# Weight conversion beside attention moved to fixed places in the program, its loads issued a period ahead, with a third raw buffer and two exchanged banks

## The chip, the core and the metric

The kernel runs on one core of a Trainium2 chip. The metric is the device time of one execution in microseconds. Three runs of the kernel before took 648.32, 651.28 and 651.58 us, median 651.28. The engines are TensorE (PE, with its weight loads shown apart as PEld), VectorE (DVE), ScalarE (ACT), GpSimd (POOL) and SyncE (SP), which issues nearly all DMAs.

## What is computed

An attention with a compressive memory feeds a gated feed-forward network (FFN). Cut to what matters:

```python
B, H, S, D = (4, 8, 576, 64)
scores = scale * q @ k^T;  causal mask;  a = softmax(scores)
local = a @ v
q_p = phi(q)                                   # phi(x) = elu(x) + 1
mem_out = (q_p @ M_prev) / (q_p . z_prev + 1e-6)
g = sigmoid(beta)                              # per head
x = g * mem_out + (1 - g) * local              # -> [2304 tokens, 512]
gate = x @ w_gate;  val = x @ w_val            # 512 -> 1536
out = (silu(gate) * val) @ w_out               # 1536 -> 512
```

Everything is float32, but the three weight matrices arrive as 64-bit floats, handed over as pairs of 32-bit words. The kernel makes 32-bit floats of them on the chip.

## The kernel before

**Attention.** Two heads form a pair, and there are 16 pairs. The loop runs n = 0 to 16; one turn is called a period here. Period n computes the scores of pair n in blocks of 128, 256, 384, 512 and 2 x 288 keys, takes row minima and exponentials of them (`exp`, ACT), and scales them (`weighed`, POOL). Beside it stands the second half of pair n-1: its weights are transposed on PE (`turned1`, `turned`; the transposed copies are called g), the memory is read (`recall`, result `mem` scaled by `w`), and values are summed (`recalled`, `values`). `leave` writes the result x in two parts: a rounded high part (`xh`, ACT) and the remainder (`xl`, DVE). q and k are split in the same way into `qh`, `ql`, `kh`, `kl`, and a product takes three matmuls (high x high, low x high, high x low). From the second pair on, `ql` and `kl` are made on POOL.

**Banks.** Four PSUM banks, s0 to s3, hold scores. Four others, tr0 to tr3, are taken in turn by `rot` for transposes, memory reads and the sums. In each period the last two takers are the pair of sums that `recalled` opens: one for token blocks 0 and 1 (`first`), one for the rest (`rest`). The sum that sits in tr2 and the one in tr3 are read by `leave` in the following period before the first long transposes (`turned(2, 0)` into tr2, `turned(2, 1)` into tr3) may overwrite them.

**Weights.** A third is a 128 x 512 piece of one weight matrix; there are 36, three (gate, value, out) for each of 12 slices f of the hidden dimension. A third is loaded raw (`raw_load`, tile `wraw`, 512 KB, two buffers), its upper words are taken through an activation (`raw_top`, ACT, tile `we`), two DVE operations make the bits of it (`we`, then `wa`), a third DVE operation joins the lower word (`wa<-wraw,wa`), ACT rounds the high part (`wgh` or `woh`) and DVE makes the low part (`wgl` or `wol`). Gate and value thirds are also written to `wdr`, out thirds to `wdo`, to be read again in the later passes. The first three thirds are made during attention, at EARLY = (1, 2, 3), the other 33 in the first pass of the FFN.

**What sets the order.** The lower-case engine names `pe, act, dve, pool` (made by `queued`) chain each instruction to the one before, so it stays in the order of the program text. Instructions on the upper-case names `ACT, DVE, SP` are placed by the framework's scheduler, by priorities. The thirds beside attention are on the upper-case names and are given a priority 200 later than their place in the text.

**FFN.** Three passes over 768 tokens each, t0 = 0, 768, 1536; a unit is one pass and one slice f, so 36 units. In the first pass a unit takes four products of 12 matmuls (`eight`), which take two banks in turn, and six groups of three (`lower`) that add the output. The two later passes use seven products. The functions that the change and the steps below touch are `raw_load`, `raw_top`, `low_part`, `third`, `pair_split`, `recalled`, the period loop and the loop over the units with its inner `some`.

Of the kernel before, what the change touches and what calls it, by code (L numbers as in the profile page):

```python
# [9 lines left out]
F32 = mybir.dt.float32  # L10
F32R = mybir.dt.float32r
I32 = mybir.dt.int32
AF = mybir.ActivationFunctionType
ALU = mybir.AluOpType
# [12 lines left out]

P_LOAD = 400
ORDER = (0, 768, 1536)
EARLY = (1, 2, 3)  # L30
P_EARLY = 200
ACT_K = (0, 1)
ON_POOL = ("q", "k")
PS_S, PS_T = 4, 4
# [9 lines left out]
def attention_moe(ctx: ExitStack, tc: tile.TileContext, qt, kt_, v, m, beta, wg, wv, wo, out):  # L44
# [61 lines left out]
        return pool.tensor_scalar(dst, src, 1.0, 0.0, op0=ALU.mult, op1=ALU.add)  # L106

    def split_lo(dst, src, hi, kind=""):
        eng = pool if kind in ON_POOL else DVE
        return eng.tensor_tensor(dst, src, hi.bitcast(F32), op=ALU.subtract)  # L110

    ident = const.tile([128, 128], F32, name="ident")
# [42 lines left out]

    held, wout = {}, {}
    thirds = [(f, j) for f in range(NF) for j in range(3)]
    raws, tops, low_parts = {}, {}, []

    def raw_load(n, after=None):  # L160
        if n < len(thirds):
            f, j = thirds[n]
            raws[n] = rot(wp, "wraw", [128, 512, 2], I32, 2)
            ld = SP.dma_start(raws[n].rearrange("p a b -> p (a b)"), (wg, wv, wo)[j][f].bitcast(I32))
            if after is not None:
                follow(ld, after, "the loads that the attention waits for go first")
# [11 lines left out]
                for i, o in enumerate((oh, ol)):  # L178
                    SP.dma_start(wdo[f, :, i], o.bitcast(F32))

    def third(act, dve, n):

        low_part(dve)
        if n >= len(thirds):
            return
        f, j = thirds[n]
        e, low = tops.pop(n), raws.pop(n)[:, :, 0]
        dve.tensor_scalar(e, e, W_TOP * 2.0**-111, -W_TOP * 2.0**-79, op0=ALU.min, op1=ALU.max)
        a = rot(wp, "wa", [128, 512], I32, 3)
        dve.tensor_scalar(a, e.bitcast(I32), 3, None, op0=ALU.logical_shift_left)  # L190
        dve.scalar_tensor_tensor(
            out=a, in0=low, scalar=29, in1=a, op0=ALU.logical_shift_right, op1=ALU.bitwise_or
        )
        if j == 0:
            held[f] = [rot(wp, f"wg{part}", [128, 1024], F32R, 2) for part in "hl"]
        if j == 2:
            wout[f] = oh, ol = [rot(wp, f"wo{part}", [128, 512], F32R, 3) for part in "hl"]
        else:
            c = slice(j * 512, j * 512 + 512)
            oh, ol = (x[:, c] for x in held[f])  # L200
            SP.dma_start(wdr[f, :, c], a.bitcast(F32))
        act.copy(oh, a.bitcast(F32))
        low_parts.append((f, j, a.bitcast(F32), oh, ol))

    with tc.tile_pool(name="sb", bufs=1, reuse_waits="tile") as sb:

# [17 lines left out]
        def pair_split(n, raw):  # L224
            qr, kr = raw
            q = [rot(sb, f"q{part}", [128, 640], F32R, NK) for part in "hl"]
            k = [rot(sb, f"k{part}", [128, 576], F32R, NK) for part in "hl"]
            early = n == 0
            (ACT.copy if n in ACT_K else split_hi)(k[0], kr)
            split_hi(q[0], qr[:, 128:768])  # L230

            def lows():
                split_lo(q[1], qr[:, 128:768], q[0], "" if early else "q")
                split_lo(k[1], kr, k[0], "" if early else "k")

            return q, k, lows

# [20 lines left out]
        class Pair:  # L258
# [128 lines left out]

            def recalled(self):

                rest, first = (rot(psT, "tr", [128, 512], F32, PS_T) for _ in range(2))  # L390
                self.av = first, rest
                y = self.mem.rearrange("p t j d -> p t (j d)")
                for t in (2, 3, 0, 1):
                    o = t % 2 * 128
                    pe.matmul(self.av[t // 2][:, o : o + 128], y[:, t], ident, start=(t % 2 == 0), stop=False, skip_group_check=True)
# [75 lines left out]
        pairs[0].load()  # L471
        gates()
        pairs[0].split()
        pairs[0].load_v()
        pairs[0].phi_parts()()
        pairs[1].load()
        pairs[0].lows()
        nothing = lambda *args: None
        ending = lambda: nothing
        for n in range(NP + 1):  # L480
# [25 lines left out]
            turned(2, 1, dve)  # L506
            exp(1, 1)
            scale = old.recall() if old else nothing
            if cur:
                cur.weighed(((0, 0), (0, 1), (1, 0), (1, 1)))  # L510
            scale()
            if after:
                after.lows()
            phi = after.phi_parts() if after else nothing
            reads = [scores(t) for t in range(2, 4)]
# [24 lines left out]
                    pairs[n + 2].load()  # L540
            if after:
                after.load_v()
            if n in EARLY:
                with later_by(P_EARLY):
                    i = EARLY.index(n)
                    raw_load(i, loads[n + 1])
                    raw_top(ACT, i)
                    third(ACT, DVE, i)
                    low_part(DVE)

        ending()()

# [1 line left out]
    with tc.tile_pool(name="stg2", bufs=1, reuse_waits="tile") as stg2, \  # L554
# [209 lines left out]
        first = units[0][0]  # L764
        for p, i, j in (("p1", 0, 0), ("p2", 0, 1), ("p7", 1, 0), ("p4", 1, 1)):
            direct(first, p, i, j)
        raw_load(3)
        raw_load(4)
        before = None
        spreads = lambda mix, *what: [  # L770
            (high if kind == "h" else low)(mix, p, k) for kind, p in what for k in range(2)
# [2 lines left out]
        for n, unit in enumerate(units):  # L774
# [5 lines left out]
            again(n)  # L780
            if whole and left:
                def some(i):
                    if i == 3:
                        raw_top(act, 3)
                    third(act, dve, i)
                    raw_top(act, i + 1)
                    raw_load(i + 2)
                for k in range(3):
                    plan[k].append(lambda i=3 * n + 3 + k: some(i))
            if n < len(units) - 1 and units[n + 1][0] != first:  # L790
# [106 lines left out]
```

## Time and profile before

| | before |
|---|---|
| median of three runs | 651.28 us |
| the profiled execution, its own time | 653.73 us |
| its span, first to last instruction | 651.8 us |
| PE busy | 627.0 us (96%) |
| DVE busy | 460.0 us (71%) |
| ACT busy | 362.7 us (56%) |
| POOL busy | 156.0 us (24%), all in the attention |
| mean granted PE clock | 0.988 |

Busy shares are means over two quite different stages: the attention ends at about 212 us, the FFN fills the rest. The end of a matmul is modelled, so a PE row can look longer than the engine was held; the starts are what to compare. A timeline row gives the start in us, the duration in us, the engine, the line, the operation, and in brackets how long the engine sat idle before it and what ended that. The granted clock is a share of full speed: 1.0 is 2.4 GHz, 0.5 is 1.2 GHz.

### The profile page before, as it was taken

The numbers are of one execution on the slowest core, as the hardware profiler recorded it, in microseconds if no ns is written. First come the engines' busy times: TensorE is split into PE (matmuls) and PEld (weight loads), VectorE is DVE, ScalarE is ACT, GpSimd is POOL, SyncE is SP. The second block draws the span as 40 slices with busy tenths as digits, with TensorE's granted clock in tenths as the row PEclk, the third lists the DMA queues.
The fourth block names the chain that finished last, engine by engine and source line by source line (L and its number), as shares of the span: only waits on it lengthen the run. The fifth ranks groups of instructions, "written<-read, shape, count | busy, mean of one in ns | idle before, by whom it ended". The sixth has DMA issues, their size and how long they took to land.

```text
span 651.8 us, 11300 instructions
## 1 busy us (share of the span) xinstructions
PE 627.0 (96%) x3912; PEld 558.4 (86%) x3912; DVE 460.0 (71%) x1151; ACT 362.7 (56%) x838; POOL 156.0 (24%) x217
## 2 busy tenths in 40 slices
PE   3889999999999899999999999999999999999997
PEld 2767878878787799999999999999999999999995
DVE  4878887878876567667686666665688756666653
ACT  6667887878874444434445565454445744445342
POOL 4667878878783000000000000000000000000000
PEclk9979999999999899999999999999999999999999
DMA  7466557554331676688765561222646533232102
GB/s 216 133 207 203 167 159 219 158 146 153 100 110 42 220 237 198 208 283 284 255 211 171 201 209 66 98 97 76 214 163 223 182 117 109 66 113 81 65 32 98
DMA packets 48744, 102.46 MB, mean 157 GB/s; under 512 B 6960, under 2 KB 16176, under 8 KB 48688
## 3 DMA queue, kind: packets, MB, share of 16 engines
q1 hardware_dynamic: 48544, 101.45, 48.0%
q8 instruction: 31, 0.51, 0.4%
q10 hardware_dynamic: 144, 0.29, 0.1%
q14 instruction: 25, 0.20, 0.1%
HBM read 74.99 MB, written 26.74 MB: 156 GB/s over the span
## 4 chain that ended last, share of the span: by engine, by line
PE 84%; DVE 5%; ACT 4%; DMA 4%; issue 2%; POOL 1%; DVEq 0%; SPq 0%; ACTq 0%; POOLq 0%
PE s L83 52%; PE tr L83 32%; ACT pl L83 3%; DMA wraw<-in_wo_dram 2%; ACT g L83 1%; DVE mem L83 1%; DMA wraw<-in_wg_dram 1%; DVE pl L83 1%; DVE w L83 1%; DMA qr<-in_qt_dram 1%; DVE rs L83 1%; POOL ps L83 0%; DMA out_dram<-pt 0%; POOL ql L83 0%; POOL kl L83 0%
## 5 line engine op out<-in xcount | busy, mean ns | idle before, releaser
L83 PE MATMUL tr<-woh,uh 128*128 128x512 f32 x144 | 57.3, 398 | 0.0
L83 PE MATMUL tr<-wol,uh 128*128 128x512 f32 x144 | 56.7, 394 | 0.0
L83 PE MATMUL tr<-woh,ul 128*128 128x512 f32 x144 | 56.5, 393 | 0.0
L83 POOL TENSOR_SCALAR pl<-pl,rs,og 128x384 f32<-128x384 f32 (+1 forms) x64 | 44.8, 715 | 29.8 <-DVE rs L83 23.8
L83 ACT ACTIVATE pl<-pl,mx 128x384 f32<-128x384 f32 (+1 forms) x64 | 42.4, 665 | 15.0 <-DVE mx L83 15.0
L83 ACT ACTIVATE zh<-zh 128x384 f32<-128x384 f32 x24 | 12.7, 530 | 67.8 <-DVE zh L83 67.8
L83 PE MATMUL tr<-g,vp 128*64 128x320 f32 (+4 forms) x448 | 48.7, 360 | 0.0
L83 PE MATMUL s<-kh,qh 64*128 64x128 f32 (+4 forms) x160 | 37.2, 389 | 11.2 <-ACT gs L142 6.9
L83 DVE TENSOR_TENSOR zv<-s,zv 128x384 f32<-128x384 f32 x24 | 13.4, 558 | 47.1 <-PE s L83 47.1
L83 PEld LDWEIGHTS tr<-g,vp 128*64 128x64 f32 x448 | 29.4, 137 | 16.9
L83 DVE CUSTOM_DVE_ANT_0 pl<-s,maskp 128x384 f32<-128x384 f32 (+1 forms) x64 | 38.1, 616 | 0.0
L83 POOL TENSOR_SCALAR ps<-ps,rs,og 128x128 f32<-128x128 f32 (+1 forms) x64 | 32.3, 518 | 14.4 <-DVE rs L83 14.0
L83 DVE COPY g<-tr 128x384 f32<-128x384 f32 (+1 forms) x64 | 32.1, 522 | 3.0 <-PE tr L83 1.8
L83 ACT ACTIVATE ps<-ps,mx 128x128 f32<-128x128 f32 (+1 forms) x64 | 28.8, 457 | 9.5 <-DVE mx L83 9.5
L83 ACT COPY g<-tr 128x384 f32<-128x384 f32 (+1 forms) x64 | 31.5, 529 | 4.3 <-DVE w L83 2.2
L83 PEld LDWEIGHTS tr<-ident,pl 128*128 128x128 f32 x224 | 24.7, 144 | 9.9 <-issue 7.3
L83 PEld LDWEIGHTS s<-kh,qh 64*128 64x128 f32 (+1 forms) x160 | 19.3, 198 | 16.2 <-issue 7.1
L83 PEld LDWEIGHTS tr<-woh,ul 128*128 128x128 f32 x144 | 27.1, 188 | 7.0 <-DVE ul L83 0.3
L83 DVE TENSOR_TENSOR tl<-tt,th 128x512 fp32r<-128x512 f32 x48 | 32.8, 684 | 0.0
L83 ACT CAST th<-tt 128x512 fp32r<-128x512 f32 x48 | 30.0, 624 | 4.8 <-DVE tt L83 2.0
L83 PE MATMUL tr<-ident,pl 128*128 128x128 f32 x224 | 32.0, 285 | 0.6 <-DVE xl L83 0.6
L83 PE MATMUL s<-kl,qh 64*128 64x128 f32 (+4 forms) x160 | 31.9, 334 | 0.7 <-DVE kl L110 0.6
(187 smaller groups left out, 1960.6 us busy)
## 6 DMA issues: line engine op xcount, KB each, us to landing
wr<-wdr SPq DMA_DIRECT2D x24, 512.0 KB, 3.3
qr<-in_qt_dram SPq DMA_DIRECT2D x16, 384.0 KB, 3.3
wraw<-in_wg_dram SPq DMA_DIRECT2D x12, 512.0 KB, 4.1
wdr<-wa SPq DMA_DIRECT2D x24, 256.0 KB, 2.7
wraw<-in_wv_dram SPq DMA_DIRECT2D x12, 512.0 KB, 3.9
wraw<-in_wo_dram SPq DMA_DIRECT2D x12, 512.0 KB, 4.5
wol<-wdo SPq DMA_DIRECT2D x24, 256.0 KB, 2.8
woh<-wdo SPq DMA_DIRECT2D x24, 256.0 KB, 3.2
```

Of the source, the lines that this page charges most:

```text
L83: ins = getattr(eng, name)(*args, **kw)
```

## The change

The conversion of a third is cut in pieces with places of their own. For the three thirds beside attention the load is issued in one period, the activation stands in the next, the two bit operations in the one after, the joining of the lower word and the high part one later, and the low part one later still, all on the chained engine names; they begin at EARLY = (2, 5, 8). Three more thirds (3, 4, 5) are loaded in periods 11, 12, 13, and the activation of third 3 is done in period 13; before, the loads of 3 and 4 stood after the attention and that activation in the first unit of the FFN. There are three raw buffers in place of two, and in the FFN loads run three thirds ahead in place of two.

In the opening, `kl` of pair 0 is made before `ql`, both stand ahead of the first phi and on the chained engine, and in period 0 the `ql` and `kl` of pair 1 go to POOL ahead of the scaling of the first blocks. In `recalled` the names `first` and `rest` are exchanged, so that `first` sits in tr2 and `rest` in tr3.

```diff
-EARLY = (1, 2, 3)
-P_EARLY = 200
+EARLY, AHEAD = (2, 5, 8), (11, 12, 13)
...
-            raws[n] = rot(wp, "wraw", [128, 512, 2], I32, 2)
+            raws[n] = rot(wp, "wraw", [128, 512, 2], I32, 3)
...
+    def third_bits(dve, n):
+        e = tops[n]
+        dve.tensor_scalar(e, e, W_TOP * 2.0**-111, -W_TOP * 2.0**-79, op0=ALU.min, op1=ALU.max)
+        wa[n] = a = rot(wp, "wa", [128, 512], I32, 3)
+        dve.tensor_scalar(a, e.bitcast(I32), 3, None, op0=ALU.logical_shift_left)
...
-            (ACT.copy if n in ACT_K else split_hi)(k[0], kr)
+            (act.copy if early else ACT.copy if n in ACT_K else split_hi)(k[0], kr)
...
             def lows():
+                if early:
+                    split_lo(k[1], kr, k[0])
                 split_lo(q[1], qr[:, 128:768], q[0], "" if early else "q")
-                split_lo(k[1], kr, k[0], "" if early else "k")
+                if not early:
+                    split_lo(k[1], kr, k[0], "k")
...
-                rest, first = (rot(psT, "tr", [128, 512], F32, PS_T) for _ in range(2))
+                first, rest = (rot(psT, "tr", [128, 512], F32, PS_T) for _ in range(2))
...
+            if n == 0:
+                after.lows()
             if cur:
                 cur.weighed(((0, 0), (0, 1), (1, 0), (1, 1)))
             scale()
-            if after:
+            if after and n:
                 after.lows()
...
-            if n in EARLY:
-                with later_by(P_EARLY):
-                    i = EARLY.index(n)
-                    raw_load(i, loads[n + 1])
-                    raw_top(ACT, i)
-                    third(ACT, DVE, i)
-                    low_part(DVE)
+            for i, at in enumerate(EARLY):
+                if n == at - 1:
+                    raw_load(i, loads[n + 2])
+                if n == at:
+                    raw_top(act, i)
+                if n == at + 1:
+                    third_bits(dve, i)
+                if n == at + 2:
+                    third_word(act, dve, i)
+                if n == at + 3:
+                    low_part(dve)
+            if n in AHEAD:
+                raw_load(len(EARLY) + AHEAD.index(n), loads[n + 2])
+                if n == AHEAD[-1]:
+                    raw_top(act, len(EARLY))
...
-        raw_load(3)
-        raw_load(4)
...
                 def some(i):
-                    if i == 3:
-                        raw_top(act, 3)
                     third(act, dve, i)
                     raw_top(act, i + 1)
-                    raw_load(i + 2)
+                    raw_load(i + 3)
```

DVE in period 0, from the reading of the 512-key scores (`pl<-s`) to the reciprocals of the sums (`rs`), before:

```order
L83 ISA pl_223,mx_149<-s_159,maskp 128x512
L188 TENSOR_SCALAR we_408<-we_408 128x512
L83 ISA pl_225,mx_149<-s_160,maskp 128x512
L190 TENSOR_SCALAR wa_411<-we_408 128x512
L83 ISA p_215,mx_149<-s_151,maskp 128x288
L191 SCALAR_TENSOR_TENSOR wa_411<-wraw_406,wa_411 128x512
L83 ISA p_215,mx_149<-s_152,mask_89,mx_149 128x288
L83 SCALAR_TENSOR_TENSOR ph_194<-qe_139,ph_194 128x640
L176 TENSOR_TENSOR wgl_415<-wa_411,wgh_414 128x512
L83 TENSOR_SCALAR rs_233<-sm_150 128x5
```

and now:

```order
L82 ISA pl_223,mx_149<-s_159,maskp 128x512
L82 ISA pl_225,mx_149<-s_160,maskp 128x512
L82 ISA p_215,mx_149<-s_151,maskp 128x288
L82 ISA p_215,mx_149<-s_152,mask_89,mx_149 128x288
L82 SCALAR_TENSOR_TENSOR ph_194<-qe_141,ph_194 128x640
L82 TENSOR_SCALAR rs_233<-sm_150 128x5
```

The four operations of the first third have left this place. They stand at the ends of periods 3, 4 and 5 now, each between the first `xl` of a period's end and the first reading of the next period's scores.

PE at the end of a period, from the transposes of the last block (`ident,p`) through the memory read (`ident,mem`) to the sums over values (`g,vp`), before:

```order
L83 MATMUL tr0_272<-ident_76,p40_215 128x128 x4
L83 MATMUL tr1_277<-ident_76,p40_215 128x128
L83 MATMUL tr2_284<-ident_76,mem0_295 128x128 x2
L83 MATMUL tr3_289<-ident_76,mem0_295 128x128 x2
L83 MATMUL tr3_289<-g10_247,vp0_132 64x256 x2
L83 MATMUL tr2_284<-ident_76,mem0_295 64x64 x2
L83 MATMUL tr2_284<-g20_248,vp0_132 64x320 x6
```

and now:

```order
L82 MATMUL tr0_272<-ident_76,p40_215 128x128 x4
L82 MATMUL tr1_277<-ident_76,p40_215 128x128
L82 MATMUL tr3_289<-ident_76,mem0_295 128x128 x2
L82 MATMUL tr2_284<-ident_76,mem0_295 128x128 x2
L82 MATMUL tr2_284<-g10_247,vp0_134 64x256 x2
L82 MATMUL tr3_289<-ident_76,mem0_295 64x64 x2
L82 MATMUL tr3_289<-g20_248,vp0_134 64x320 x6
```

The order of the matmuls is the same; tr2, which ACT empties into g just before, is now written second, and tr3, which DVE empties, first.

ACT at the start of the FFN, from its first gate activation (`zg`) to the second (`zh`), before:

```order
L83 ACTIVATE zg_2524<-s_152 128x384
L83 ACTIVATE we_566<-wraw_564 128x512
L83 CAST wgh_2530<-wa_411 128x512
L83 ACTIVATE we_408<-wraw_406 128x512
L83 CAST uh_2549<-zg_2524 128x384
L83 CAST wgh_2530<-wa_569 128x512
L83 ACTIVATE we_566<-wraw_564 128x512
L83 ACTIVATE zh_2573<-s_152 128x384
```

and now:

```order
L82 ACTIVATE zg_2527<-s_152 128x384
L82 CAST wgh_2532<-wa_701 128x512
L82 ACTIVATE we_553<-wraw_849 128x512
L82 CAST uh_2551<-zg_2527 128x384
L82 CAST wgh_2532<-wa_1137 128x512
L82 ACTIVATE we_993<-wraw_1285 128x512
L82 ACTIVATE zh_2575<-s_152 128x384
```

One activation (`we`) has left the stretch, and the two that remain read raw buffers that were loaded in periods 12 and 13.

## Rows read from the trace of the kernel before

**Rows 1.** Chain that ended last, shares of the span.
```profile
PE 84%; DVE 5%; ACT 4%; DMA 4%; issue 2%; POOL 1%; DVEq 0%; SPq 0%; ACTq 0%; POOLq 0%
```

**Rows 2.** Windows: stretch, its length, busy us of engines, granted clock, DMA.
```profile
33.70:51.15 17.45, 14.30 (x111) 11.60 (x107) 12.42 (x44) 11.07 (x31) 10.76 (x14) 0.80 0.62 197
63.17:203.24 140.07, 138.97 (x1261) 112.18 (x1262) 115.32 (x431) 109.80 (x310) 113.13 (x153) 1.00 0.48 144
220.55:223.77 3.22, 0.17 (x2) 0.00 (x1) 1.12 (x3) 1.25 (x3) 0.00 (x0) 0.85 0.76 263
223.77:229.66 5.89, 5.89 (x18) 5.89 (x19) 4.23 (x9) 2.38 (x5) 0.00 (x0) 0.50 0.79 258
```

**Rows 3.** Timeline of PE, periods 0 to 2, rows with a wait.
```profile
16.74 0.47 PE L83 MATMUL s<-kh,qh 64*128 64x128 f32 x2 [2.35 <-DVE mx L83]
39.47 2.54 PE L83 MATMUL tr<-mm,ph 128*128 128x130 f32 x10 [2.92 <-ACT g L83]
```

**Rows 4.** Timeline of DVE, periods 0 to 2.
```profile
15.36 0.62 DVE L188 TENSOR_SCALAR we<-we 128x512 f32<-128x512 f32 x1 [1.75 <-ACT we L171]
16.51 1.01 DVE L190 TENSOR_SCALAR wa<-we 128x512 int32<-128x512 int32 x1
20.20 0.16 DVE L83 TENSOR_SCALAR rs<-sm 128x5 f32<-128x5 f32 x1
...
31.17 1.49 DVE L176 TENSOR_TENSOR wgl<-wa,wgh 128x512 fp32r<-128x512 f32 x1
```

**Rows 5.** Timeline of ACT, periods 0 and 2.
```profile
14.66 0.67 ACT L171 ACTIVATE we<-wraw 128x512 f32<-128x512 f32 x1 [0.55 <-DMA wraw<-in_wg_dram]
38.37 0.68 ACT L171 ACTIVATE we<-wraw 128x512 f32<-128x512 f32 x1 [2.90 <-DMA wraw<-in_wo_dram]
```

**Rows 6.** Timeline of POOL, the first pairs, and one steady period.
```profile
15.66 1.58 POOL L83 TENSOR_TENSOR kl<-kr,kh 128x576 fp32r<-128x576 f32 x1
...
30.68 1.43 POOL L83 TENSOR_TENSOR kl<-kr,kh 128x576 fp32r<-128x576 f32 x1
...
97.36 2.80 POOL L83 TENSOR_SCALAR pl<-pl,rs,og 128x384 f32<-128x384 f32 x4 [1.45 <-DVE rs L83]
```

**Rows 7.** Timeline of PE and PEld in one steady period.
```profile
98.96 0.87 PE L83 MATMUL tr<-ident,ps 128*128 128x128 f32 x6
99.82 0.84 PE L83 MATMUL tr<-ident,pl 128*128 128x128 f32 x6
100.51 1.28 PE L83 MATMUL tr<-mm,ph 128*128 128x130 f32 x10
...
104.87 0.71 PE L83 MATMUL tr<-ident,p 128*128 128x128 f32 x5
105.66 1.16 PE L83 MATMUL tr<-ident,mem 128*128 128x128 f32 x8
...
99.79 0.64 PEld L83 LDWEIGHTS tr<-ident,pl 128*128 128x128 f32 x6 [0.20 <-issue]
...
105.66 0.97 PEld L83 LDWEIGHTS tr<-ident,mem 128*128 128x128 f32 x8 [0.32 <-ACT g L83]
```

**Rows 8.** Timeline of DVE, then ACT, around the change of period.
```profile
98.76 0.29 DVE L83 CUSTOM_DVE_ANT_0 ps<-s,maskp 128x128 f32<-128x128 f32 x1 [1.26 <-POOL pl L83]
...
99.19 0.48 DVE L83 TENSOR_TENSOR xl<-tr,xh 128x320 fp32r<-128x320 f32 x1
...
98.19 0.43 ACT L83 CAST xh<-tr 128x320 fp32r<-128x320 f32 x1 [1.18 <-PE tr L83]
```

**Rows 9.** Timeline of PE, ACT and DVE at the start of the FFN.
```profile
223.77 0.69 PE L83 MATMUL s<-xp1h,wgh 128*128 128x384 f32 x1 [3.05 <-ACT zh L83]
...
222.68 0.66 ACT L83 ACTIVATE we<-wraw 128x512 f32<-128x512 f32 x1 [1.91 <-DMA wraw<-in_wo_dram]
...
217.89 0.69 DVE L83 TENSOR_TENSOR wgl<-wa,wgh 128x512 fp32r<-128x512 f32 x1 [0.22 <-ACT wgh L83]
218.50 0.42 DVE L83 TENSOR_SCALAR we<-we 128x512 f32<-128x512 f32 x1
```

More of the change, by code (lines that the diff above doesn't have):

```diff
@@ L108, in split_lo @@
     def split_lo(dst, src, hi, kind=""):
-        eng = pool if kind in ON_POOL else DVE
+        eng = pool if kind in ON_POOL else dve
         return eng.tensor_tensor(dst, src, hi.bitcast(F32), op=ALU.subtract)
@@ L157, in attention_moe @@
     thirds = [(f, j) for f in range(NF) for j in range(3)]
-    raws, tops, low_parts = {}, {}, []
+    raws, tops, wa, low_parts = {}, {}, {}, []
     def raw_load(n, after=None):
@@ L179, in low_part, with third_word @@
                     SP.dma_start(wdo[f, :, i], o.bitcast(F32))
[L181 to L185, printed above, removed]
+    def third_bits(dve, n):
[3 more added lines that the diff above has]
+        dve.tensor_scalar(a, e.bitcast(I32), 3, None, op0=ALU.logical_shift_left)
+    def third_word(act, dve, n):
         f, j = thirds[n]
[L187 to L190, printed above, removed]
+        tops.pop(n)
+        a, low = wa.pop(n), raws.pop(n)[:, :, 0]
         dve.scalar_tensor_tensor(
@@ L203, in third @@
         low_parts.append((f, j, a.bitcast(F32), oh, ol))
+    def third(act, dve, n):
+        low_part(dve)
+        if n < len(thirds):
+            third_bits(dve, n)
+            third_word(act, dve, n)
     with tc.tile_pool(name="sb", bufs=1, reuse_waits="tile") as sb:
@@ L473, in attention_moe @@
         pairs[0].split()
+        pairs[0].lows()
         pairs[0].load_v()
@@ L476, in attention_moe @@
         pairs[1].load()
-        pairs[0].lows()
         nothing = lambda *args: None
@@ L542, in attention_moe @@
                 after.load_v()
-            if n in EARLY:
-                with later_by(P_EARLY):
-                    i = EARLY.index(n)
-                    raw_load(i, loads[n + 1])
-                    raw_top(ACT, i)
-                    third(ACT, DVE, i)
-                    low_part(DVE)
+            for i, at in enumerate(EARLY):
[8 more added lines that the diff above has]
+                if n == at + 3:
+                    low_part(dve)
+            if n in AHEAD:
+                raw_load(len(EARLY) + AHEAD.index(n), loads[n + 2])
+                if n == AHEAD[-1]:
+                    raw_top(act, len(EARLY))
         ending()()
```

## The prediction

> **What bounds the kernel now.** First the chain of waits: 84% of it is PE [rows 1], so a step counts only where PE stands still or runs slow. The windows by stage say where. Twelve steady periods, 63.17 to 203.24, last 140.07 us, 11.67 each; period 2 (33.70 to 51.15) lasts 17.45 at a granted clock of 0.80; at the start of the FFN PE does nothing for 3.22 us and then runs 18 matmuls in 5.89 us at clock 0.50, which is 1.2 GHz [rows 2]. From 229.66 on the chain names only PE, and I leave that part as it is. So there are three places to look at: the first three periods, the 14 period changes that follow, the start of the FFN.
>
> In the first periods the timelines tell the cause. In period 0 DVE stands 1.75 us before `we`, waiting for ACT's `we`, which waited for the load of the first third; the bit operation `wa` then takes 1.01 us [rows 4, 5]. The read of the 512-key scores stands behind, and PE waits 2.35 us for it before it can write period 1's scores [rows 3]. In period 2 ACT stands 2.90 us for the load of the third third, with the copies g that PE needs behind it, and PE loses 2.92 us [rows 3, 5]. At the start of the FFN ACT stands 1.91 us for `wraw`, `zh` is behind it in the queue, and PE waits 3.05 us for `zh` to free a bank [rows 9].
>
> **The change part by part.**
>
> *First periods.* Period 0 loses on DVE the wait of 1.75, `we` 0.62, `wa` 1.01, and the joining and the low part, for which I take the 0.69 of an equal low part later [rows 4, 9]: 1.75 + 0.62 + 1.01 + 2 x 0.69 = 4.8 us ahead of `rs` at 20.20. ACT loses less, a `we` of 0.67 behind a wait of 0.55 and a rounding, and its exponentials feed `rs`; so I take 4.0 of the 4.8. What could be late next is `kl` of pair 1, which POOL ended at 15.66 + 1.58 = 17.24 [rows 6]; it now stands ahead of the scaling of the first blocks and comes the sooner by that. Period 1 loses a low part of 1.49 and a joining (0.69), of which I take 2.0 for the chain; the two bit operations there I count at nothing, since PE was behind anyway. Together 6.0 us at the start of period 2, with 2.35 (PE's own wait) and 7.0 as ends. Period 2 then has no third in it: 17.45 - 11.67 = 5.8 us. Sum **-11.8**, ends -5.8 (only period 2 mends, or the two halves mend half each) and -12.8.
>
> *Exchange of first and rest.* At the end of a period PE needs tr2 and tr3. Five transposes begin at 104.87; at the pace of the next period's `pl` (six in 100.51 - 99.82 = 0.69, 0.115 each) they are done at 105.44, yet the memory read begins at 105.66, and the weight load before it waits 0.32 for ACT's g [rows 7]. That g is the copy out of tr2. Now tr3 goes first, which DVE empties earlier, and tr2 is wanted two matmuls later: 0.22 us gone per period. Likewise six `ps` transposes take 99.82 - 98.96 = 0.86 where six `pl` of the same shape take 0.69, and the weight load after them waits 0.20 with no cause named [rows 7]. I put that on `xl` of the sum that sits in tr2: it begins at 99.19 and lasts 0.48, to 99.67, and PE goes on at 99.82 [rows 7, 8]. After the exchange tr2 holds the other sum, whose `xl` was done in the period before, and the later one is wanted three transposes on, 0.35 us later: 0.17 us gone. What is late next is PE itself; POOL's `pl` scalings of 0.70 begin at 97.36 and have two done at about 98.8, and the DVE chain behind the memory read moves with PE. So 0.39 x 14 = **-5.5**. Ends: 0, if the next wait stands right behind, and -7.3, if the whole idle time of the weight loads (0.52) goes.
>
> *The thirds at written places.* ACT gets one operation of 0.62 to 0.67 in seven periods, just before `xh` of 320 columns, where it stood 1.18 us waiting for PE [rows 8]: hidden, with about 0.1 us to spare after the exchange, since 1.18 - 0.39 = 0.8. If that cover were gone, `xh` and `xl` and through them tr3 would be late by the same amount. DVE gets nine insertions ahead of the first read of the new scores, where it stood 1.26 us, 0.87 after the exchange [rows 8]: three pairs of bit operations (2 x 0.42) and six single ones (0.69), of which either would just fit alone [rows 9]. They are not alone: POOL scales `pl` there, four operations in 2.80, beginning in the same moment [rows 6]. Beside POOL `wa` took 1.01 where 0.42 is the size of such an operation later; a low part took 1.49 where the same takes 0.69, and it ran out only after POOL's `kl` (30.68 + 1.43 = 32.11; 31.17 + 1.49 = 32.66) [rows 4, 6, 9]. If each waits out the rest of a scaling (0.5) and the second bit operation a whole one (0.70), a pair costs 0.5 + 0.42 + 0.7 + 0.42 - 0.87 = 1.2 and a single 0.5 + 0.69 - 0.87 = 0.3, in all 3 x 1.2 + 6 x 0.3 = 5.4. Behind the waiting DVE operation stand the reads of the scores, behind them ACT's exponentials and g, for which PE waits. The ends are 0 and 5.4; below nothing is excluded, as no work leaves this place. I take **+2.5**, about the middle, because `xl` at 99.19, though it reads a bank, ran beside POOL's scalings at 0.48 for 320 columns, 1.5 ns each, against 1.35 for a low part without POOL (0.69 for 512) [rows 6, 8, 9].
>
> The Trainium skill, "SBUF — State Buffer", section "SBUF: two separate sides", speaks against this part: VectorE in a two-port mode or with two SBUF inputs and a GpSimd operation hold a shared port pair as an exclusive lock, for the whole instruction, and the other blocks. The 1.49 above agrees. By that rule, an estimate, the term would be nearer 5.4 than 2.5, and the sum 2.9 us longer.
>
> *SP's queue.* Each raw load now stands behind a load of k in a place where the next thing waits for PE; a write to `wdr` stands ahead of `xh`'s. I count these issues at nothing: nobody reads them within a period. If they were late, POOL's splits of the next pair would be, and PE's scores with them.
>
> *Start of the FFN.* Third 3 has its activation already, thirds 4 and 5 their loads. ACT's queue to `zh` has no load to wait for; `zh` still follows a rounding that needs two DVE conversions, for which I leave 0.3 us, an allowance. So 3.05 - 0.3 = 2.75 of the wait goes, and with so short a gap I expect the clock to stay: 18 matmuls at 1.00 in place of 0.50 give back 5.89 / 2 = 2.9 at most [rows 2, 9]. Together **-5.5** (rounded from 5.65), ends 0 and -5.95. Three loads ahead in place of two costs nothing while PE has no other wait in the FFN.
>
> **Sum.** -11.8 - 5.5 + 2.5 - 5.5 = -20.3. The profiled execution took 653.73 us, so 633.4; it lies 2.45 us above the median of the runs, 651.28, and I take the same distance off: **631 us**.
>
> **The rivals.**
> 1. *The exchange brings nothing.* For it: 12 periods of exactly 11.67 may have more than one loop of that length, and POOL is busy for 113 of 140 us [rows 2]. Against it: both gaps on PE have a named or timed cause [rows 7]. 631 + 5.5 = 636.5.
> 2. *The insertions aren't hidden.* Each of the nine pays for itself in full beside POOL, at 1.01 to 1.49 as in the first periods, about 1.2 x 9 = 10.8 in place of 2.5: 639. For it: the three slow rows of before [rows 4]. Against it: there POOL ran two-input subtractions, and here it scales [rows 6]. The lock told of above, from the page "SBUF — State Buffer" of the Trainium skill, would work in this direction; the rows have it in two cases, so its chance stands at 0.15.
> 3. *The first periods mend by half.* PE, the opening loads or POOL's `kl` hold period 1, and only period 2's 5.8 is won: 637. Were the thirds not the cause at all, so that the change misses what it moves, 631 + 11.8 = 643.
> 4. *Slower: the FFN's first pass stalls again and again.* With loads three ahead, a load of `wraw` stands in SP's queue behind a read of `wdr` that waits for its own write; then ACT waits for `wraw` in each of 11 units, as it did once [rows 9], and each time PE pays 3.05 + 2.9 = 5.95. The start is not won either: 631 + 5.5 + 5.95 per unit, so it is slower than before from the third stalled unit on (654.4), and 702 with all eleven. Against it: a raw buffer more, and a load issued a third earlier than the one that was late.
>
> **How the numbers follow.** Forecast 0.50; rival 1 0.17; rival 2 0.15; rival 3 0.09 and its extreme 0.03; rival 4 0.03; all insertions hidden and both gaps gone whole (-7.3; 627) 0.03. The range takes the forecast's own ends for the unknown insertions and the exchange, and the first three rivals: 623 to 641. About 0.5% (3.3 us) is what a measurement of this kernel can tell from no change. All but rival 4 and a rest of 0.02 lie below 648: faster 0.95, same 0.02, slower 0.03.
>
> **What would show it.** Right: PE's scores of period 2 begin near 28 us in place of 33.7 and those of period 3 less than 12 us later; the steady stretch without thirds runs at 11.3 us a period, the wait for g before the memory read is gone, and `pl` follows `ps` without a gap; DVE's inserted rows are below 0.8 us; the gap before the FFN's second unit is under 0.5 us and the clock there 1.00. Wrong: periods of 11.67 as before (the exchange), inserted rows above 1 us with a longer period at 3, 4, 5, 6 and so on (the insertions), a PE wait above 2 us before 30 us (the opening), or any wait for `zh` or `zg` in the first pass (rival 4).

## The result, and the profile after

The changed kernel takes 635.24 us (median; runs 634.19 to 635.36) against 651.43 for the kernel before on the same chip, a ratio of 0.975 [0.969, 0.980]. It is faster, inside the range, and 4.2 us above the predicted 631. The profiled execution took 635.18 us, so from profile to profile the change brought 18.55 us where 20.3 were forecast.

The page of the kernel after: busy time, the granted clock in 40 slices, and the chain by engine, which answers to [rows 1].

```profile
PE 619.0 (98%) x3912; PEld 554.1 (87%) x3912; DVE 462.2 (73%) x1151; ACT 360.2 (57%) x838; POOL 159.1 (25%) x217
PEclk9999999999999999999999999999999999999999
PE 94%; DVE 3%; DMA 1%; ACT 1%; issue 1%; SPq 0%; DVEq 0%
```

PE's share of the chain rose from 84 to 94%. The windows after answer to [rows 2]: period 2, periods 4 to 13, the FFN up to its second unit, and the first matmuls of that unit (columns: stretch, length, busy us of PE, PEld, DVE, ACT and POOL, granted clock, share of the DMA engines, GB/s).

```profile
29.74:41.28 11.54, 11.45 (x109) 9.38 (x105) 9.98 (x36) 9.81 (x27) 9.74 (x14) 1.00 0.46 140
52.89:167.43 114.54, 114.36 (x1056) 93.90 (x1052) 105.79 (x372) 94.56 (x266) 102.22 (x131) 1.00 0.61 193
199.11:207.97 8.86, 8.59 (x52) 8.27 (x48) 5.98 (x12) 5.34 (x9) 0.00 (x0) 1.00 0.69 249
207.97:211.02 3.05, 3.04 (x17) 3.05 (x18) 1.80 (x5) 1.76 (x4) 0.00 (x0) 1.00 0.76 220
```

Period 2 has become an ordinary one, ten periods last 11.45 each where they lasted 11.67, and the 18 matmuls that took 5.89 us at clock 0.50 take 3.05 at 1.00. PE's timeline after, around the places of [rows 3, 7, 9]:

```profile
13.44 0.61 PE L82 MATMUL s<-kh,qh 128*128 128x288 f32 x1 [1.92 <-DVE mx L82]
29.74 0.33 PE L82 MATMUL s<-kh,qh 64*128 64x128 f32 x2
30.63 0.87 PE L82 MATMUL tr<-ident,ps 128*128 128x128 f32 x6
31.34 0.82 PE L82 MATMUL tr<-ident,pl 128*128 128x128 f32 x6
36.78 0.71 PE L82 MATMUL tr<-ident,p 128*128 128x128 f32 x5
37.33 1.06 PE L82 MATMUL tr<-ident,mem 128*128 128x128 f32 x8
207.97 0.44 PE L82 MATMUL s<-xp1h,wgh 128*128 128x384 f32 x1 [0.28 <-ACT zh L82]
```

Both gaps that the exchange was to close are closed: the `ps` transposes go over into `pl` after 0.71 us (0.86 before), the memory read follows five transposes after 0.55 (0.79 before). The wait for `zh` fell from 3.05 to 0.28. Period 2 begins at 29.74, not near 28.

By the starts of the first score matmuls of each period, and of the FFN, in the two profiles:

| stretch | forecast | before | after | measured |
|---|---|---|---|---|
| up to the start of period 2 | -6.0 | 33.71 | 29.74 | -3.97 |
| period 2 | -5.8 | 17.36 | 11.54 | -5.82 |
| period 3 to the FFN (exchange -5.5, thirds +2.5) | -3.0 | 161.06 | 157.83 | -3.23 |
| FFN to its second unit, and 18 matmuls | -5.5 | 11.64 + 5.89 | 8.86 + 3.05 | -5.62 |

That is -18.64 of the -18.55. The third line looks right, but not as it was made up. Forecast were 11.28 us for a period without inserted work (called empty below) and more for those with it. Measured are 11.54 to 11.63 for the four without (2, 3, 13, 14), hardly less than the 11.67 of before, and 11.33 to 11.48 for the nine with. So the exchange opened both gaps and the period gave most of it back elsewhere. Where, PE's timeline of period 13 shows: ahead of the 288-key scores. In before they began 0.85 us after the eight `pl` transposes:

```profile
103.15 1.09 PE L83 MATMUL tr<-ident,pl 128*128 128x128 f32 x8
104.00 0.38 PE L83 MATMUL s<-kh,qh 128*128 128x288 f32 x1
```

and now

```profile
160.63 1.09 PE L82 MATMUL tr<-ident,pl 128*128 128x128 f32 x8
161.89 0.40 PE L82 MATMUL s<-kh,qh 128*128 128x288 f32 x1 [0.17 <-DVE mx L82]
```

it is 1.26, and PE waits for DVE's reading of scores. Back along DVE's queue, the same period on DVE and on POOL:

```profile
159.71 0.66 DVE L82 TENSOR_SCALAR rs<-sm 128x4 f32<-128x4 f32 x1
160.41 0.18 DVE L82 RECIPROCAL rs<-rs 128x4 f32<-128x4 f32 x1
160.51 0.86 DVE L82 TENSOR_TENSOR mem<-tr,w 128x384 f32<-128x384 f32 x2
...
159.62 0.73 POOL L82 TENSOR_SCALAR qh<-qr 128x640 fp32r<-128x640 f32 x1
```

The first row adds 1e-9 to four sums per partition, 4 columns, and takes 0.66 us; it ends at 160.37, POOL's `qh` at 160.35. In before the same addition began 0.07 us before POOL's operation ended, and so waited for next to nothing (DVE, then POOL):

```profile
102.23 0.11 DVE L83 TENSOR_SCALAR rs<-sm 128x4 f32<-128x4 f32 x1
...
101.57 0.73 POOL L83 TENSOR_SCALAR qh<-qr 128x640 fp32r<-128x640 f32 x1
```

The reason that the experiments test is therefore: the exchange moves DVE's chain forward against POOL's, the addition falls under a POOL operation and waits it out, and DVE's readings, for which PE waits, come late by that. The rival is the prediction's own sentence that what is late next is PE itself, and later a second one: that any operation more in this chain costs as much.

### The profile page after: what moved, and what is told of

It is laid out like the page before. It is cut to its first block, busy times and chain, and to the rows that moved or that the text cites. A ratio compares the mean times of both kernels' runs of the same rounds, so it can differ in the third digit from the quotient of the medians.

```text
span 633.3 us, 11316 instructions
## 1 busy us (share of the span) xinstructions
PE 619.0 (98%) x3912; PEld 554.1 (87%) x3912; DVE 462.2 (73%) x1151; ACT 360.2 (57%) x838; POOL 159.1 (25%) x217
## 4 chain that ended last, share of the span: by engine, by line
PE 94%; DVE 3%; DMA 1%; ACT 1%; issue 1%; SPq 0%; DVEq 0%
PE s L82 58%; PE tr L82 36%; DMA kr<-in_kt_dram 1%; DVE pl L82 1%; DVE rs L82 1%; DVE mem L82 0%; DVE w L82 0%; ACT ps L82 0%; SPq L256 0%; DVE wa L82 0%; SPq L221 0%; DVE p L82 0%; DVE pt L82 0%; ACT wgh L82 0%; DVE g L82 0%
## 5 line engine op out<-in xcount | busy, mean ns | idle before, releaser
L82 POOL TENSOR_SCALAR pl<-pl,rs,og 128x384 f32<-128x384 f32 (+1 forms) x64 | 49.2, 782 | 24.6 <-DVE rs L82 21.9
L82 DVE SCALAR_TENSOR_TENSOR zg<-s,zg 128x384 f32<-128x384 f32 x36 | 20.0, 557 | 19.3 <-PE s L82 18.5
L82 DVE TENSOR_TENSOR zg<-s,zp 128x384 f32<-128x384 f32 x24 | 13.4, 558 | 25.1 <-ACT bh L82 19.8
```

The lines of the kernel that those rows point to most:

```text
L82: ins = getattr(eng, name)(*args, **kw)
```

## The experiments

Medians in us, with the ratio to the kernel before on the same chip. That kernel's own medians there lie between 650.13 and 652.35, so differences of about 1 us are read from the periods and not from the medians.

| kernel | median | ratio |
|---|---|---|
| no_rs_add | 630.52 | 0.967 [0.965, 0.969] |
| no_exchange | 642.60 | 0.985 [0.983, 0.987] |
| no_ex_no_add | 635.91 | 0.976 [0.973, 0.978] |
| exchange_alone | 645.38 | 0.990 [0.987, 0.994] |
| early_old | 643.35 | 0.989 [0.986, 0.992] |
| ahead_undone | 635.38 | 0.977 [0.974, 0.979] |
| opening_undone | 636.99 | 0.979 [0.977, 0.982] |
| load_first | 632.76 | 0.972 [0.970, 0.975] |
| two_raw | 635.84 | 0.977 [0.975, 0.979] |
| three_recips | 635.36 | 0.976 [0.974, 0.979] |
| two_recips | 631.35 | 0.969 [0.967, 0.972] |
| spread | 629.27 | 0.967 [0.964, 0.969] |

**The addition, with the exchange and without.** no_rs_add is the changed kernel without the addition (1e-9 to sums that are at least 1; the other kernels that leave it out say so in their expectations):

```diff
-                dve.tensor_scalar(rs, self.sm[:, c : c + n], 1.0e-9, None, op0=ALU.add)
-                dve.reciprocal(rs, rs)
+                dve.reciprocal(rs, self.sm[:, c : c + n])
```

> The changed kernel without the addition of 1e-9 in rs; the reciprocal reads the sums directly. Theory 1 (port): that addition, 4 columns on DVE, takes 0.5 to 0.66 us per period because POOL has an operation in flight, and PE's 288-key scores stand behind it; without it a period without an insertion falls from 11.62 to about 11.3 and those with one from 11.46 to about 11.35, in all 2 to 4 us faster than the changed kernel (631 to 633 us). Theory 2 (PE): PE is at its own floor and the wait is covered; the same time within 1 us, the operations that remain only start earlier.

Measured 630.52, 4.7 us less. That is just below the 631 to 633 of the wait for POOL; the theory of PE as the bound falls. PE's timeline of period 13 without the addition, and the rows of DVE and POOL beside it:

```profile
156.89 1.09 PE L82 MATMUL tr<-ident,pl 128*128 128x128 f32 x8
157.74 0.38 PE L82 MATMUL s<-kh,qh 128*128 128x288 f32 x1
...
155.97 0.12 DVE L82 RECIPROCAL rs<-sm 128x4 f32<-128x4 f32 x1
...
155.60 0.74 POOL L82 TENSOR_SCALAR qh<-qr 128x640 fp32r<-128x640 f32 x1
```

The reciprocal runs in the middle of `qh` and takes 0.12. The step to the 288-key scores is 0.85 again, and empty periods last 11.12 to 11.13. Of the 4.7 us, 1.9 lie ahead of period 2 (27.88 in place of 29.74), which is less firm than the rest, as the next section shows. no_exchange puts the two sums back into their banks:

```diff
-                first, rest = (rot(psT, "tr", [128, 512], F32, PS_T) for _ in range(2))
+                rest, first = (rot(psT, "tr", [128, 512], F32, PS_T) for _ in range(2))
```

> The changed kernel with first and rest as before. By the prediction's term the exchange was worth 5.5 us, so 640.7. By theory 1 (the port wait of rs gave back most of it) it is worth what the periods show, about 0.2 x 13: 637.5 to 638.5, with periods of 11.67 and more and a wait for g before the memory read.

Measured 642.6, above both. Its empty periods last 11.64 to 11.68, so there the exchange is worth only 0.07; those with inserted work last 12.05 to 12.17. Beside the rest of the change the exchange is worth 7.4 us, most of it because without it these nine periods last 0.4 to 0.5 us longer than the empty ones. no_ex_no_add has both edits.

> The changed kernel with first and rest as before and without the addition in rs. Theory 1: without the exchange rs did not wait for POOL, so leaving it out gives at most 0.1 x 14 = 1.4 us against the kernel with first and rest as before. If leaving it out gives 3 us here too, the gain is that of one operation less on DVE and not of the port.

635.91, 6.7 less than no_exchange. The expectation allowed 1.4 and called 3 us a sign against the wait for POOL, so it was missed by far. What it had wrong is that without the exchange the addition does not wait. That holds in the empty periods, where it takes 0.11 to 0.14 and leaving it out saves 0.1 (11.56). In the nine with inserted work it takes 0.41 to 0.63 and ends with POOL's `qh`, as here in no_exchange:

```profile
81.78 0.62 DVE L82 TENSOR_SCALAR rs<-sm 128x4 f32<-128x4 f32 x1
...
81.64 0.72 POOL L82 TENSOR_SCALAR qh<-qr 128x640 fp32r<-128x640 f32 x1
```

Without it these nine last 11.56 to 11.77, and one 12.0. The profiled executions differ by 4.6 of the 6.7 us: that of no_ex_no_add took 637.95, the longest of its four runs, so where the rest lies is not shown. With the addition gone, the exchange is worth 11.56 - 11.12 = 0.44 per period; 0.39 was forecast. Over the whole kernel it is then 5.4 us (635.91 to 630.52); 5.5 was forecast. exchange_alone is the kernel before with that one line exchanged.

> The kernel before with only first and rest exchanged. By the prediction's term 5.5 us faster than before (646). By theory 1 the periods go from 11.67 to 11.62 and the whole to about 650.5, with rs at 0.5 to 0.66 us.

645.38: by the number that is the prediction's 646 and not the theory's 650.5. By the periods it is the theory: the steady ones are 11.63 to 11.67, as before, but period 3, with the same program, lasts 11.11, and period 14 lasts 11.13 (addition 0.15). The two kinds beside each other, on DVE and on POOL:

```profile
51.66 0.13 DVE L83 TENSOR_SCALAR rs<-sm 128x4 f32<-128x4 f32 x1
62.77 0.70 DVE L83 TENSOR_SCALAR rs<-sm 128x4 f32<-128x4 f32 x1
...
51.73 0.74 POOL L83 TENSOR_SCALAR qh<-qr 128x640 fp32r<-128x640 f32 x1
62.72 0.73 POOL L83 TENSOR_SCALAR qh<-qr 128x640 fp32r<-128x640 f32 x1
```

In period 3 the addition begins 0.07 us ahead of `qh`, in the next 0.05 behind it. It is 0.57 longer there, and the period 0.55 longer. Most of the gain lies where the theory did not look: 3.1 us in period 2 (17.36 to 14.25, clock 1.00 in place of 0.80), 3.2 at the start of the FFN (PE waits 1.78 for `zh` in place of 3.05, and the clock behind it is 1.00 in place of 0.50). Why the wait for `zh` and the one for g in period 2 (2.92 to 0.74) fell these runs don't say.

**Is it the addition, or one operation more?** three_recips puts two more reciprocals in its place, two_recips one (the same line twice).

```diff
-                dve.tensor_scalar(rs, self.sm[:, c : c + n], 1.0e-9, None, op0=ALU.add)
+                dve.reciprocal(rs, self.sm[:, c : c + n])
                 dve.reciprocal(rs, rs)
+                dve.reciprocal(rs, rs)
```

> The addition of 1e-9 to the sums is left out and two more reciprocals are put behind the first (the result is again 1/sum), so DVE has one small operation more per call than the changed kernel has. Port theory (only the addition waits for POOL; a reciprocal of this size does not): 630.5 to 632 us, each reciprocal below 0.2 us, also beside POOL. Rival (the gain of leaving the addition out is a shorter chain of DVE operations, whatever they are): 635.5 to 637 us.

635.36: just under the rival's price, against the theory, though no reciprocal takes more than 0.19. Its empty periods are 11.30, those with inserted work up to 11.91. So the chain does pay for length; the question was left whether the first operation more does.

> The addition of 1e-9 is left out and the reciprocal of the sums is issued twice into the same place, so DVE has as many operations here as the changed kernel, in the same order. Two more reciprocals cost 4.8 us (635.36 against 630.52 of the kernel with one). Theory (an operation in this chain costs by its own length, and the addition costs its wait for POOL on top): half of the 4.8, so about 633 us, 632.3 to 633.7; the other half of the 4.7 that the addition costs is the wait for POOL. Rival (the price is that of one more operation in the chain, and the wait beside POOL is hidden): 634.6 to 635.8 us, as the changed kernel.

631.35, below the theory's range and far below the rival's. With as many operations as the changed kernel has, 3.9 of the 4.7 us are gone: that is the wait for POOL. One reciprocal more costs 0.8 (empty periods still 11.12), the second 4.0; the halves are not equal, since the first fits in slack. The copy that DVE makes behind the memory's read shows it. Here it is in period 13 with one reciprocal, two and three, which begins at 152.00, 152.71 and 156.49:

```profile
158.02 0.69 DVE L82 COPY g<-tr 128x512 f32<-128x512 f32 x1
...
158.73 0.69 DVE L82 COPY g<-tr 128x512 f32<-128x512 f32 x1
...
162.65 0.69 DVE L82 COPY g<-tr 128x512 f32<-128x512 f32 x1
```

It begins 6.02, 6.02 and 6.16 into the period. With one reciprocal DVE stands 0.09 us before it; the second uses that up, the third shifts the copy, the readings of scores behind it come 0.13 to 0.19 later, and the empty period is 0.18 longer. Of the 4.0 us, more than 1 lies ahead of period 2. The groups of the tile `rs` (min, median, max in ns) in the kernel after, and without the addition, show the wait itself:

```profile
L82 DVE TENSOR_SCALAR rs<-sm x32: 106/172/894, 11.8 to 189.2; 128x4 f32<-128x4 f32 x16, 128x5 f32<-128x5 f32 x16
```

```profile
L82 DVE RECIPROCAL rs<-sm x32: 118/176/192, 12.0 to 184.4; 128x4 f32<-128x4 f32 x16, 128x5 f32<-128x5 f32 x16
```

**The opening.** early_old has the first three thirds at EARLY = (1, 2, 3) again, placed by the scheduler.

```diff
-EARLY, AHEAD = (2, 5, 8), (11, 12, 13)
+EARLY, AHEAD = (1, 2, 3), (11, 12, 13)
...
+                with later_by(200):
+                    raw_load(i, loads[n + 1])
+                    raw_top(ACT, i)
+                    third(ACT, DVE, i)
+                    low_part(DVE)
```

> The changed kernel with the first three thirds made as before, in periods 1 to 3 where the scheduler puts them. By the prediction's terms it loses 11.8 and wins back the 2.5 of the insertions: 644.5. By what the exchange alone showed (period 2 at 14.25 and not 17.4, since the exchange frees PE from the g behind the late load) only about 7 us are lost: 641 to 642.5.

643.35, between the two expectations: moving the thirds is worth 8.1 us. PE's wait in period 2 is back nearly as in [rows 3], so the exchange does not free PE from it, as the second expectation had it:

```profile
38.74 1.38 PE L82 MATMUL tr<-mm,ph 128*128 128x130 f32 x10 [2.96 <-ACT g L82]
```

The clock stays at 1.00 behind it, though, and period 2 lasts 14.95 where it lasted 17.36.

opening_undone has `kl` and `ql` of the first two pairs made where they were before.

```diff
-            if n == 0:
-                after.lows()
...
-            if after and n:
+            if after:
```

> The changed kernel with the opening as before: ql before kl and both behind phi for pair 0, and the lows of pair 1 on POOL behind the scaling of the first blocks. By the prediction, which put kl of pair 1 at 17.2 otherwise, period 2 begins 1 to 2 us later: 636.5 to 637.5. By the port theory the first rs, which took 0.89 us beside POOL's kl, is at 0.1 to 0.2 here, and that pays for part: 635 to 636.

636.99, within what the prediction's reading gave, so this part is worth some 1.7 us (the intervals of the ratios overlap). PE waits for the `kl` of pair 1 that it moved:

```profile
17.81 0.48 PE L82 MATMUL s<-kl,qh 64*128 64x128 f32 x2 [2.85 <-POOL kl L82]
```

The first addition is short, as the other reading had it (0.17), but the next one now meets `kl`: it takes 1.36 and ends at 17.78, `kl` at 17.75.

load_first, without the addition, also issues the loads of pair 1 ahead of v and the memory.

```diff
+        pairs[1].load()
...
-        pairs[1].load()
```

> The kernel without the addition in rs, and with the loads of q and k of pair 1 issued ahead of the loads of v and of the memory. In the opening ACT waits for k of pair 1, which lands at 9.7 us after being issued at 4.1. If that load sets the opening, it lands 1 to 2 us sooner and period 2 begins 0.5 to 1.5 us sooner: 629 to 630. If the opening hangs on ACT's exponentials alone, nothing changes: 630.5.

632.76, slower by 2.2 than no_rs_add, which neither expectation allowed. POOL gets its input sooner, and its `ql` now lies beside DVE's small operations of the opening (DVE, then POOL):

```profile
9.05 1.49 DVE L144 TENSOR_SCALAR gt<-gt 128x8 f32<-128x8 f32 x1
...
8.54 1.98 POOL L82 TENSOR_TENSOR ql<-qr,qh 128x640 fp32r<-128x640 f32 x1
```

Eight columns take 1.49 us and end at 10.54, `ql` at 10.52; the first reading of scores follows at 10.57.

**The start of the FFN.** ahead_undone takes back the loads in periods 11 to 13 and the activation, two_raw the third buffer and one load.

```diff
-            if n in AHEAD:
-                raw_load(len(EARLY) + AHEAD.index(n), loads[n + 2])
-                if n == AHEAD[-1]:
-                    raw_top(act, len(EARLY))
...
+        raw_load(3)
+        raw_load(4)
+        raw_load(5)
```

> The changed kernel without the three loads in periods 11 to 13 and the activation in 13; loads 3, 4, 5 are issued after the attention, still with three raw buffers. By the prediction's term 5.5 us slower (640.7), with a wait of PE for zh before the second unit and a clock of 0.50 behind it. If three buffers alone were enough, the wait would be below 1 us and the time 635 to 636.

```diff
-EARLY, AHEAD = (2, 5, 8), (11, 12, 13)
+EARLY, AHEAD = (2, 5, 8), (12, 13)
...
-            raws[n] = rot(wp, "wraw", [128, 512, 2], I32, 3)
+            raws[n] = rot(wp, "wraw", [128, 512, 2], I32, 2)
...
-                    raw_load(i + 3)
+                    raw_load(i + 2)
```

> Two raw buffers in place of three, loads of thirds 3 and 4 issued in periods 12 and 13, the activation of third 3 still in period 13, and in the FFN each load one third later. Theory of the prediction (the activation and the loads made ahead end the stall at the start of the FFN): 635 to 636 us, no wait of PE above 0.6 us before its second unit, clock 1.00 there. Rival (the third buffer ended it, since with two the load of the next third must wait for the copy out of the buffer before): 638 to 641 us, PE waits 1 to 3 us for zh near the start of the FFN, and the clock falls behind the longer of these waits.

635.38 and 635.84: neither brings the loss back. The first unit's end on PE, of ahead_undone and of two_raw:

```profile
207.97 0.44 PE L82 MATMUL s<-xp1h,wgh 128*128 128x384 f32 x1 [1.03 <-ACT zh L82]
```

```profile
208.11 0.44 PE L82 MATMUL s<-xp1h,wgh 128*128 128x384 f32 x1 [0.30 <-ACT zh L82]
```

In ahead_undone the scheduler itself moved a load up into the attention, since a buffer was free (issued at 132.5), so the edit didn't undo what it should; 0.76 us of wait come back (9.62 us to the second unit in place of 8.86) and the clock stays at 1.00 behind it. In its profile the opening ran 0.9 us faster than after's with the same program, which hides them in the total. With two buffers and the work ahead the wait is 0.30 and the first unit takes 8.88. So the work made ahead is enough and the third buffer isn't needed; the third buffer with one load early does nearly as much.

**A version that beats both.** spread leaves the addition out and gives each step of a third a period of its own.

```diff
-EARLY, AHEAD = (2, 5, 8), (11, 12, 13)
+EARLY, AHEAD = (1, 6, 11), (11, 12, 14)
...
-                    third_bits(dve, i)
+                    third_clip(dve, i)
...
-                    third_word(act, dve, i)
+                    third_shift(dve, i)
+                if n == at + 3:
+                    third_join(dve, i)
+                if n == at + 4:
+                    third_high(act, i)
+                if n == at + 5:
                     low_part(dve)
```

> Without the addition of 1e-9, and with each step of a third (clip, shift, joining, high part, low part) in a period of its own, the thirds begun in periods 1, 6 and 11, and the activation of third 3 in period 14. In the kernel without the addition the periods with two bit operations last 0.2 us longer than the ones with none, and those with a joining and a copy 0.32 longer. Theory (it is two insertions in the same place that don't fit, each by itself does): 629 to 629.5 us, all periods from 3 on between 11.1 and 11.2. Rival (any insertion costs what it costs, wherever it stands): 630 to 631 us.

629.27 (628.64 to 629.75), as the theory had it. All periods from 3 to 12 last 11.12, and 13 lasts 11.34; in no_rs_add the two bit operations cost 0.18 to 0.45 and joining with high part 0.32. The ratios of the two kernels overlap, so the 1.2 us between their medians are shown by the periods (the FFN begins at 193.22 in place of 194.36) rather than by the totals.

## Why the prediction was right, and where it was not

*First periods, -11.8 forecast, -9.8 measured.* The mechanism was right: the thirds are the cause (early_old), and period 2 mends by 5.8 as worked out. The 6.0 by the start of period 2 were 4.0. What was late next was named, `kl` of pair 1, but only as something for which PE might wait. Its cost came in another way: placed ahead of the scaling, it lies beside the addition (DVE, then POOL, of the kernel after).

```profile
11.83 0.89 DVE L82 TENSOR_SCALAR rs<-sm 128x4 f32<-128x4 f32 x1 [2.01 <-ACT ps L82]
...
11.30 1.39 POOL L82 TENSOR_TENSOR kl<-kr,kh 128x576 fp32r<-128x576 f32 x1
```

The addition ends at 12.72, `kl` at 12.69, and PE's wait for the readings behind is the 1.92 shown above; without the addition it is 0.21 and period 2 begins at 27.88, 5.83 us earlier than before. Of the 1.86 us between these two kernels 0.80 are there at the start of period 1 (15.23 and 14.43). Nearly all the rest goes with PE's pace, which in the opening of every profile is about half of the later one (in the kernel after six `ps` transposes take 1.54 us in period 1 and 0.87 in period 2). Ten matmuls of period 1 in the kernel after, in ahead_undone and two_raw, whose opening is the same program:

```profile
19.75 2.37 PE L82 MATMUL tr<-mm,ph 128*128 128x130 f32 x10
...
19.57 1.28 PE L82 MATMUL tr<-mm,ph 128*128 128x130 f32 x10
...
19.93 1.94 PE L82 MATMUL tr<-mm,ph 128*128 128x130 f32 x10
```

Without the addition they take 1.35. The three begin period 2 at 29.74, 28.85 and 29.79, so up to 1 us of the opening hangs on when PE becomes quick. The profiles give the granted clock as 1.00 all along there, and what sets the moment is open.

*Exchange, -5.5 forecast.* Both gaps were real and rightly sized: 0.44 per period without the addition, 0.39 forecast. The step that failed is "What is late next is PE itself". The sum took DVE's chain as moving with PE, and did not ask what POOL runs when the chain comes 0.4 us sooner: the addition waits there, and the empty periods are 11.54 to 11.63 with it and 11.12 without. The end "0, if the next wait stands right behind" came true in the periods without inserted work (11.67 before, 11.54 to 11.63 now). As a whole rival 1 is wrong: in place the exchange is worth 7.4.

*Thirds at written places, +2.5 forecast.* Against the same kernel's empty periods they cost nothing, they give back 0.1 to 0.3 us each. Of the inserted operations only the second bit operation is longer beside POOL (0.61 to 0.70 in place of 0.43); the others keep their size. A low part and the addition in one such period, then POOL:

```profile
75.43 0.68 DVE L82 TENSOR_TENSOR wgl<-wa,wgh 128x512 fp32r<-128x512 f32 x1
79.67 0.50 DVE L82 TENSOR_SCALAR rs<-sm 128x4 f32<-128x4 f32 x1
...
75.37 3.33 POOL L82 TENSOR_SCALAR pl<-pl,rs,og 128x384 f32<-128x384 f32 x4 [1.16 <-DVE rs L82]
79.47 0.67 POOL L82 TENSOR_SCALAR kh<-kr 128x576 fp32r<-128x576 f32 x1
```

The low part takes 0.68, as without POOL; it is POOL that pays, 3.33 for four scalings where it was 2.80 [rows 6]. So POOL comes later, by 0.5 us here, the addition meets `kh` 0.2 us or more after its start instead of `qh` 0.1 to 0.2 after its start, and takes 0.24 to 0.50 in place of 0.58 to 0.66. That the inserted work shortens periods is an effect of the missed wait: without the addition the nine cost 1.8 us together (sum of the periods over 11.12), near the forecast 2.5. The Trainium skill, "SBUF — State Buffer", section "SBUF: two separate sides", which the prediction weighed here, says that VectorE in a two-port mode, or with two SBUF inputs as a low part has them, and GpSimd take the shared port pair for a whole instruction, whichever starts first, and the other waits. The traces agree that either can be the one that waits (0.66 on DVE, 3.33 on POOL). That the first to start wins does not show at this distance: POOL's row of 3.33 begins 0.06 us before DVE's. The prediction put the rule to the nine large operations and not to the smallest one of the period, where it decided.

*Start of the FFN, -5.5 forecast, -5.62 measured.* Right in both halves, the wait and the clock. The cause was given as the work made ahead; two_raw agrees, ahead_undone adds that a free buffer with one load early nearly suffices.

*SP's queue* and rival 4: no stall came, PE is busy 98% of the span. Rival 2 fell. Without the exchange the nine periods cost some 4 us (0.4 to 0.5 each), but only 1.1 of it is left when the addition is gone too, so that is its wait again and not the price of the inserted operations.

*The last step.* Of the 4.2 us between 631 and 635.24, 1.8 are the sum. The other 2.45 are the distance from the profiled run to the median, which was carried over from before. It does not carry: the runs of the kernel before spread from 648.32 to 655.12, those of the changed kernel from 634.19 to 635.36, and its profiled run lies on its median. And some of the agreement is luck: the third line of the table is the difference of two terms that were both off. The chances, by the way, add up to 1.00 without the "rest of 0.02" that the prediction speaks of.

## What to carry to other kernels

When a change moves one engine's chain earlier, lay its new start times beside what POOL runs then, the smallest operations too: what a small DVE operation paid here is what was left of POOL's operation, not its own size. Prefer there a form that did not wait in the trace (here the reciprocal), or drop the operation. Carry the distance between a profiled run and its median over only if both kernels scatter alike.

## What the runs showed that was not expected

- The addition, a `TENSOR_SCALAR` of 4 or 5 columns on DVE, took 0.10 to 1.36 us. In the eight profiles that have it, it stands 256 times. The 95 that took more than 0.2 us all began while a POOL operation ran and ended 0.02 to 0.03 us after the end of one; none that began outside one took more than 0.17. A `RECIPROCAL` of the same size in the same place took 0.12 to 0.18.
- Another DVE operation waits for POOL in the same way, `ph<-qe,ph` of 640 columns: it takes 0.82 alone, and at 14 of its 16 places in the kernel after 0.84 to 1.20, always ending 0.68 us after POOL's `kl`. In period 13 of two_recips it takes 1.58 and the period lasts 11.12 all the same, as in no_rs_add with 0.82. So here such a wait cost time only where PE stood behind it.
- In the kernel before the clock fell to 0.50 in PE's wait of 2.92 us in period 2; in early_old it stayed at 1.00 through one of 2.96 us at the same place. These runs don't say why.
